# Transposing transfers by pairs and by whole weights in a kernel of a state-space branch and a linear-attention branch

## The chip, the cores and the metric

The kernel runs on one core of a Trainium2 chip. The metric is the device time of one execution in microseconds (us). The profile is that of one execution.

## The reference

The input `x` is 2048 rows (time) of 512 features. Two branches are computed from it and mixed by a gate per row. Cut to what matters:

```python
g = sigmoid((x * gate_w).sum(-1))
# A: a diagonal state-space model with 512 complex states
Bu = einsum("bld,pd->blp", x, B_bar)          # B_bar from B_re, B_im, Lambda, dt
h_t = Lam_bar * h_{t-1} + Bu_t                # over 2048 steps
y = 2 * einsum("blp,dp->bld", h, C).real + x * Dskip
# B: linear attention, 32 heads of 16
q, k, v = split(x @ wqkv)
phi(u) = concat(softmax(u @ w_phi), softmax(-u @ w_phi))      # 32 features per head
kv = phi(k)^T v;  z = sum(phi(k));  o = (phi(q) kv) / (phi(q) z + 1e-6)
out = g * y + (1 - g) * (o @ wo)
```

## The kernel before, in words

**Tiles and order.** The rows of `x` are cut into 16 tiles of 128 rows. A tile holds every eighth row, so that tile `ti` belongs to residue `r = ti // 2` of the time step modulo 8. `xT` holds `x` transposed, one transposing transfer per tile. Nothing is scheduled by the compiler: `ORDER` is a written list of tokens, and each token runs one generator up to its next `yield`. So the list fixes the order of instructions on TensorE (PE), VectorE (DVE), ScalarE (ACT) and the issuing order of SyncE (SP). `@n` gives the PSUM banks, `:D` sends an eviction to DVE instead of ACT. An engine runs its list strictly in order; semaphores make it wait for data.

**State-space branch.** `N` (`st_N`) loads B into `Bn`, real parts in partitions 0 to 63 and imaginary ones in 64 to 127, as eight blocks `t` of 64 states. `R{t}` (`st_BT`, L291) transposes one block into `BT`, four squares of 128x128, 128 KB of bf16. `g{r}{j}` (`st_g`, L614) multiplies `xT` by blocks `2j` and `2j+1` and evicts to `uv`. `z` scans along time, `h` (`st_h`, L685) adds the carried state and writes `HM`, `HE` and `H7`. C is read transposed by `C{0..7}` (`st_C`, L299), one quarter of C_re or C_im each, into `CA`, which lies in the space of `HM` before `h` writes it. `J` (`st_J`, L304) copies `CA` into `X1` and `X2`, in eight transfers, and `c{t}` (`st_c`, L603 and L607) scales and adds these into `C2r` and `C2i`. The two temporaries of a `c` sum, `mtmp[t % 4]`, lie in the space of `phT0[:, t % 4]`. `y` (`st_y`, L734) multiplies states by C.

**Attention branch.** `W` and `f` fold the key weight with `w_phi`; `Q{j}` (`st_Q`, L295) transposes a quarter of the query weight out of DRAM into `WTq`, `w` (L434) folds it. `k`, `v`, `q` are the projections. The features are made in groups of up to four tiles: `x`, `n` and `e` (maxima, minima, exponentials), then `s` (`feat_sum`: sums, logarithms, ratio). For queries, `feat_sum` also transposes the features into `phT`: per tile one transposing transfer of eight squares (256 KB, L579), or, for tiles 14 and 15 (`PH_PE`), PE transposes. The query groups are A (tiles 0 to 3, tokens `sA`, target `phT0`) and 1 to 3 (tokens `S1` to `S3`). `o{n}` (L753) multiplies the transposed features of tile n by the key-value sums in two halves, ACT takes logarithm and exponential of the denominators (`ld`, `rd`), DVE writes `on` (L761), and SP transposes `on` into `oT` (128 KB, L775; the last four on PE). `t{n}` (L782) adds `oT` times `wo` to the open sum of `y{n}` and sends the tile out (L790). The tokens run in the order o0, o2, o3, o1, then 4 to 9, 11, 10, 12, 14, 13, 15.

**SP's queue.** Nearly all transfers are issued by SP, in the order of the list. Each holds one of eight semaphores, handed round, so that a transfer waits for the one eight before it.

Of the kernel before, what the change touches and what calls it, by code (L numbers as in the profile page):

```python
# [31 lines left out]
g30 g50 n4 x4 e3 e3 g41@0 g50 n4 R7 s2 g21@4 s2 g70 s2 C7 e3 g31@3 e3 s3 g62@2 C4 g70 g70 z0 g11@7 a2 z0 s3 g41 z0 a2
a2 s3 C6 g21 g62 C2 C1 g11 g11 C0 J0 w0@6 w1@0 J2 J2 a2 g22@4 J0 w2@2 x4 s3 J1 g31 w1 w0 w3@7 g22 g31 z0 z0 z0 s3 w2
s3 n4 z0 z0 w3 g61@0 g51@6 g51 g61 g02@4 g51 e4 g02 g71@3 g71 g71 g71 q3@2 s3 g12@7 g12 e4 q2@0 z0 g12 z1 q3 q1@6 q1
q0@4 q2 z1 z0 h50@3 z1 z1 g42@7 q0 z1 z1 v10@26 h50 xA z1 h10@0 e4 e4 z1 g42 nA s4 g32@4 v10 g32 a3 g52@3 g32 h60@7 c2
xA s4 c4 O g52 xA c4 R6 z1 z1 v9@26 s4 h10 g52 nA g72@4 g72 c4 h60 v9 a3 J3 g03@3 v11@26 c2 c2 s4 g72 g72 c0 c0 nA
g63@0 z2 z2 v12@74 a3 nA v11 a3 xA g03 z2 z2 z2 z2 xA nA s4 J3 g63 g23@2 c5 s4 v12 g23 h51@6 g13@3 g13 g13 z2 z2 c0 z2
z2 eA g43@0 g43 eA v14@74 v14 J1 h51 s4 g33@2 g33 h52@3 g33 h12@0 g53@6 eA g53 g53 h12 h11@7 h11 h52 eA sA g73@4 g73
g73 g73 v13@26 v13 q10@0 z3 c6 z3 c5 sA z3 z3 v15@73 z3 a4 a4 a4 v15 z3 q10 q5@4 a4 Y z3 h31@0 q5 sA h30@4 z3 q9@2 h31
q13@6 h31 q9 h33@0 h61@7 Y q13 h30 sA sA c5 h62@3 z3 z3 h30 h61 sA Y Y h22@5 q4@2 h62 q4 h33 q15@6 q11@7 h22 h20@4 h20  # L40
h32@2 h32 sA sA c1 q11 h13@1 h13 h32 q14@3 h40@5 h33 c3 h53@7 h42@4 sA h42 h53 c1 c1 sA h21@2 c3 h21 q6@0 q6 q15 c6
q7@1 h63@4 h63 q8@7 h03@0 c3 q7 c6 h40 sA c7 h41@6 h41 y6@2 c7 h03 h03 h43@4 h43 y2@1 h02@5 c7 sA h23@6 h23 h01@0
h00@4 END q8 G X1 y6 y6 q14 y2 N1 X1 h00 h00 N1 y2 h02 h02 X1 N1 G h01 o0@6 y0@7 o0 o0@3 h01 o2@4 o2 X1 o2@5 o2 o2 N1
y5@6 o0 y3@0 X1 N1 y5 X2 o0 o1@4 E1 o2 y0 o2 o0 E1 E1 E1 X2 y1@5 y1 y3 y3 o1 G N2 X2 N2 X2 o0 N2 X2 o3@3 o3 o3@4 S1 o3
o3 G S1 N2 S1 t2 o3 S1 o3 t2 t2:A q12@3 q12 N2 S1 S1 o1@4 o1 o1 o1 o1 S1 S1 E2 S1 y0 y4@1 y9@3 y8@4 y8 y8 X3 E2 E2 S1
S1 S1 N3 X3 E2 t3 X3 X3 X3 S2 N3 t0 t0 t0:A S2 t3 S2 y1 t1 t1 y5 y9 y9 o4@7 o4 o4@0 o4 y4 o4 o4 o4 o5@5 o5 o5@7 o5 o5
y13@0 S2 S2 o6@5 o6 o6@7 o6 o6 y13 N3 y7@5 y7 N3 y7 y13 o5 S2 S2 N3 E3 o5 o6 o6 S2 S2 E3 E3 o7@7 o7:D y4 t4 t4:D t5
o7@7 S2 S2 E3 S3 t5 S2 S3 S3 o7 o7 o7 t6 y11@1 y11 o7 t6 o8@6 o8 o8@7 o8 o8 S3 S3 o8 y12@2 o9@6 o9 o9@7 o8 y11 y12 y12
y10@6 o9 o9 o9 o11@7 o11 o9 S3 S3 y10 y10 o11@7 t7 o11 o11 t7 t8 S3 S3 o11 o11 S3 t8 S3@7 S3:D S3@5 S3 t9 t9 t1:A
o10@4 y15@7 o10:D o10@5 o10:D t8 o10 o10 o10 y15 o12@4 o12:D o12@3 t4 o14@5 o12 o12 o12 t5 o14 t11 o14@4 o14:D o14 o14  # L50
t11 y14@3 t9:A o13@5 o13 o12@4 o12:D y14 o13@1 o13 o13 o15@4 o15:D o15@5 o15 o15 t12 t3:A t10 o13 o13@1 o15 t6:A t11
# [19 lines left out]
def kernel(  # L71
# [145 lines left out]
    WTq = HMf[:, 0:KT * D].rearrange("p (k d) -> p k d", k=KT)  # L217
    CA = HMf[:, KT * D:KT * D + 2 * PT * D].rearrange("p (a k d) -> p a k d", a=2, k=PT)
    BD = pAC.tile([P, HG, P], BF16, name="BD")
    BT = pAC.tile([P, KT, NT2, P], BF16, name="BT")  # L220
    T2c = pAC.tile([P, PT, NC], BF16, name="T2c")
    T2s = pAC.tile([P, PT, NC], BF16, name="T2s")
    uv = [pAC.tile([P, 7, 2, NC], BF16, name=f"uv{j}") for j in range(PT)]
# [63 lines left out]
        nc.sync.dma_start(out=Bn[ri * 64:(ri + 1) * 64, :, :], in_=(A_B_re, A_B_im)[ri].rearrange("(t p) d -> p t d", p=64))  # L287
        yield

    def st_BT(t):  # L290
        nc.sync.dma_start_transpose(out=BT[:, :, t, :], in_=Bn[:, t, :])  # L291
# [252 lines left out]
    def feat_sum(p, L, nm, small, ph=None, row0=0):  # L544
        EE = live["EE", p]
        E5 = EE.rearrange("p l hh s (f hl) -> p l (hh s) f hl", f=Dh)
        sm = small().tile([P, 4, 2 * NB, 1, 4], F32, name=f"sm{nm}1", bufs=2)[:, 0:L]
        yield from tree(small(), E5, L, ALU.add, f"sm{nm}", ("sm", p), last=sm, groups=2 * NB)
        lg = small().tile([P, 4, 2 * NB, 1, 4], F32, name=f"lg{nm}", bufs=1)[:, 0:L]
        aexp(out=lg, in_=sm, func=ACT.Ln)  # L550
        yield
        if ph is None:
            rc = small().tile([P, 4, 2 * NB, 1, 4], BF16, name=f"rc{nm}", bufs=2)[:, 0:L]
            aexp(out=rc, in_=lg, func=ACT.Exp, scale=-1.0)
            yield
# [12 lines left out]
        yield
        dst = ph()
        for u in range(L):  # L570
            if row0 + u in PH_PE:
# [7 lines left out]
            nc.sync.dma_start_transpose(out=dst(u), in_=EE[:, u].rearrange("p m s f -> p (m s f)"))  # L579
# [30 lines left out]
    def st_g(r, j):  # L610
        pg = bank([P, 2, NC], F32, "pgq")
        for h in range(2):
            for kt in range(KT):
                MM(out=pg[:, h, :], lhsT=BT[:, kt, 2 * j + h, :], rhs=xT[:, kt, r * NC:(r + 1) * NC], start=(h == 0 and kt == 0),  # L614
                   stop=(r % 2 == 0 and kt == KT - 1), skip_group_check=True)
# [249 lines left out]
```

## Time and profile before

| What | Value |
|---|---|
| time, median of 2 runs | 156.8 us (156.07 and 157.53) |
| span of the profiled execution, first to last instruction | 153.7 us |
| busy: PE, DVE, ACT, POOL | 145.5, 131.0, 136.7, 12.9 us |
| transposing transfers on SP: xT, BT, Q, C, phT, oT | 16, 8, 4, 8, 14, 12 |
| instructions | 3412 |

The profiled execution's own time is not listed apart from the two runs. The span lies 2.4 us below the faster and 3.8 us below the slower of them, and 3.1 us below their median. In the profile, PE is matmuls and PEld the loading of their weights, which overlaps with them; `L753` is a line of the kernel; `phT<-EEq` is an instruction that writes `phT` and reads `EEq`; SPq is an issue by SP.

### The profile page before, as it was taken

To read this page: it belongs to the slowest core of one execution; us is meant where nothing else is said; L and a number is where in the kernel's file an instruction comes from. 1 tells how busy PE (TensorE), PEld (TensorE's weight loads), DVE (VectorE), ACT (ScalarE), POOL (GpSimd) and SP (SyncE) were. 2 spreads that over 40 slices of the span, in tenths; PEclk is the share of its full clock that TensorE was granted. 3 is DMA by queue.
4 is the path that set the end of the run, shared out by engine and by line. 5 is a ranking of instruction groups with operands and counts; after the bars stand their busy time and mean duration, and the time that the engine had idled before them with its cause. 6 is when DMAs were issued, how large, how long until landed. Compare 5 with 4: busy or idle time off the path is not lost.

```text
span 153.7 us, 3412 instructions
## 1 busy us (share of the span) xinstructions
PE 145.5 (95%) x1238; PEld 99.7 (65%) x1254; DVE 131.0 (85%) x302; ACT 136.7 (89%) x322; POOL 12.9 (8%) x43
## 2 busy tenths in 40 slices
PE   7799999999999999999999999999999899999990
PEld 7656665886899858889876565554545455555550
DVE  3599999999999999999999999999999858445510
ACT  3599999999999999999999999999798897577672
POOL 8258800000000000000000000000000000000000
PEclk9999999999999999999999999999999999999998
DMA  4788995544474379960000006603139938667633
GB/s 117 162 220 121 213 171 102 102 86 92 101 102 100 80 146 205 237 133 0 2 4 2 0 0 134 125 18 68 33 82 118 215 80 194 141 118 172 211 123 102
DMA packets 48737, 17.03 MB, mean 111 GB/s; under 512 B 42064, under 2 KB 48720, under 8 KB 48720
## 3 DMA queue, kind: packets, MB, share of 16 engines
q1 hardware_dynamic: 47008, 15.36, 50.6%
q10 hardware_dynamic: 1552, 1.44, 2.9%
q8 instruction: 10, 0.16, 0.5%
q0 software_dynamic: 160, 0.01, 0.2%
q14 instruction: 7, 0.06, 0.1%
HBM read 2.64 MB, written 2.10 MB: 31 GB/s over the span
## 4 chain that ended last, share of the span: by engine, by line
ACT 48%; PE 31%; DMA 8%; DVE 6%; issue 3%; POOL 2%; ACTq 0%; POOLq 0%
PE py L734 12%; ACT EEk L140 12%; ACT uv L121 9%; PE py L782 6%; ACT vx L121 5%; PE pq L478 5%; ACT Xq L121 5%; ACT phT L603 4%; PE ph L685 3%; ACT va L121 3%; DMA phT<-EEq 3%; DMA oT<-on 3%; PE pn L753 2%; DMA vec_n<-in_A_log_dt_dram 2%; ACT EEq L140 2%
## 5 line engine op out<-in xcount | busy, mean ns | idle before, releaser
L614 PE MATMUL pgq<-xT,BT 128*128 128x256 bf16 x256 | 31.5, 272 | 0.0
L614 PEld LDWEIGHTS <-BT 128*128 128x128 bf16 x256 | 24.7, 98 | 3.5
L140 ACT ACTIVATE EEk<-EEk 128x1024 bf16<-128x1024 bf16 x20 | 21.3, 1099 | 0.0
L478 PEld LDWEIGHTS <-xT 128*128 128x128 bf16 x128 | 12.2, 97 | 11.0 <-issue 0.2
L121 ACT CAST uv<-pgq 128x512 bf16<-128x512 f32 x28 | 16.7, 638 | 0.0
L492 PE MATMUL pv<-Wv,xT 128*128 128x256 bf16 (+1 forms) x128 | 16.5, 273 | 0.1
L478 PE MATMUL pq<-Wq,xT 128*128 128x512 bf16 x60 | 15.2, 379 | 0.2
L782 PE MATMUL py<-Wo,oT 128*128 128x512 bf16 x59 | 14.7, 379 | 0.6 <-DMA oT<-on 0.3
L478 PE MATMUL pk<-Wk,xT 128*128 128x512 bf16 x60 | 14.9, 379 | 0.2
L492 PEld LDWEIGHTS <-xT 128*128 128x128 bf16 x128 | 12.5, 98 | 3.1 <-issue 0.2
L786 ACT ACTIVATE ot<-py,G 128x512 bf16<-128x512 f32 x15 | 9.8, 684 | 2.9 <-PE py L782 2.4
L140 ACT ACTIVATE EEq<-EEq 128x1024 bf16<-128x1024 bf16 x12 | 11.8, 1084 | 0.3 <-DVE EEq L535 0.3
L603 ACT ACTIVATE phT<-X,dgB 128x512 bf16<-128x512 bf16 x16 | 11.1, 751 | 0.0
L140 ACT ACTIVATE ld<-pn 128x16 f32<-128x16 f32 x32 | 6.4, 204 | 5.2 <-PE pn L753 5.0
L121 ACT CAST vx<-pv 128x256 bf16<-128x256 f32 x32 | 10.7, 435 | 0.0
L121 ACT CAST nu<-pn 128x256 bf16<-128x256 f32 x26 | 10.0, 400 | 0.0
L556 DVE TENSOR_TENSOR EEk<-EEk,rck 128x4096 bf16<-128x4096 bf16 (+1 forms) x5 | 9.3, 1860 | 0.1
L121 ACT CAST Xq<-pq 128x512 bf16<-128x512 f32 x16 | 9.0, 604 | 0.4 <-PE pn L753 0.4
L782 PEld LDWEIGHTS <-oT 128*128 128x128 bf16 x64 | 5.7, 98 | 5.7 <-DMA oT<-on 0.5
L753 PEld LDWEIGHTS <-phT 128*128 128x128 bf16 x128 | 6.4, 97 | 4.6 <-DMA phT<-EEq 1.3
L761 DVE TENSOR_TENSOR on<-nu,rd 128x512 bf16<-128x512 bf16 x16 | 6.6, 422 | 2.6 <-ACT rd L140 2.1
L519 DVE TENSOR_TENSOR smk<-smk 128x512 bf16<-128x512 bf16 (+4 forms) x18 | 8.1, 449 | 0.1
(179 smaller groups left out, 322.9 us busy)
## 6 DMA issues: line engine op xcount, KB each, us to landing
X<-HM SPq DMA_DIRECT2D x8, 256.0 KB, 4.7
out_dram<-ot SPq DMA_DIRECT2D x9, 128.0 KB, 2.2
out_dram<-ot ACTq DMA_DIRECT2D x7, 128.0 KB, 2.0
C2r<-in_B_wqkv_dram ACTq DMA_DIRECT2D x2, 256.0 KB, 3.5
Wv<-in_B_wqkv_dram SPq DMA_DIRECT2D x1, 512.0 KB, 4.0
Bn<-in_A_B_im_dram SPq DMA_DIRECT2D x1, 512.0 KB, 5.5
Bn<-in_A_B_re_dram SPq DMA_DIRECT2D x1, 512.0 KB, 5.9
Wo<-in_B_wo_dram SPq DMA_DIRECT2D x1, 512.0 KB, 5.9
```

Of the source, the lines that this page charges most:

```text
L121: nc.scalar.copy(out=out_ap, in_=in_ap)
L140: ins = nc.scalar.activation(**kw)
L478: MM(out=pt[:], lhsT=xT[:, kt, ti * P:(ti + 1) * P], rhs=W[:, kt, :], start=(kt == 0), stop=(kt == KT - 1))
L492: MM(out=pv[c][:], lhsT=xT[:, kt, ti * P:(ti + 1) * P], rhs=Wvg[:, kt, c * hd:(c + 1) * hd + c], start=(kt == 0), stop=(kt == KT - 1))
L519: VT(out=dst, in0=cur[:, :, :, 0:n, :], in1=cur[:, :, :, n:2 * n, :], op=op)
L556: VT(out=E5, in0=E5, in1=rc.to_broadcast([P, L, 2 * NB, Dh, 4]), op=ALU.mult)
L603: nc.scalar.mul(out=t_, in_=x_, mul=c_)
L614: MM(out=pg[:, h, :], lhsT=BT[:, kt, 2 * j + h, :], rhs=xT[:, kt, r * NC:(r + 1) * NC], start=(h == 0 and kt == 0), stop=(r % 2 == 0 and k ...
L734: MM(out=py[:], lhsT=hs(r, t, slice(a * P, (a + 1) * P)), rhs=C2B[t], start=(t == 0), stop=False)
L753: MM(out=pn[:, 4 * m:4 * m + 4, :].rearrange("p h e -> p (h e)"), lhsT=ph[:, 4 * hf + m, :], rhs=KVm[:, 4 * hf + m, :], start=(m == 0), st ...
L782: MM(out=py[:], lhsT=oT[:, g, :], rhs=Wo[:, g, :], start=False, stop=(g == HG - 1))
L786: nc.scalar.mul(out=ot[:], in_=py[:], mul=G[:, ti:ti + 1])
```

## The change

- BT is transposed by pairs of blocks: one transfer of eight squares for `2j` and `2j+1`. Its layout becomes `[P, NT2, KT, P]`; each square read by PE is as contiguous as before.
- C is transposed in two transfers (C_re, C_im), each of sixteen squares, 512 KB.
- The query weight is transposed in one transfer of sixteen squares.
- Query features are transposed by two tiles, sixteen squares, 512 KB: 0-1, 2-3, 4-5, 6-7, 8-9, 10-11 and 12-13.

That is 4 + 6 + 3 + 7 = 20 transposing transfers fewer, with the same bytes. In the list, tokens of transfers that no longer exist are left out, and everything else keeps its order. Q stands where the first quarter stood, the BT pairs where R0, R3, R5 and R7 stood, C_im where its first quarter stood and C_re where its first quarter stood. A feature pair stands where the transfer of its later tile or a place between stood: 0-1 in the place of tile 1, 2-3 in that of tile 3, 12-13 in that of tile 13. With that, SP issues `oT` of tile 11 ahead of the pair 12-13, where it stood between 12 and 13; the other pairs keep their neighbours on SP. The lists of PE, DVE and ACT keep their order.

```diff
-    BT = pAC.tile([P, KT, NT2, P], BF16, name="BT")
+    BT = pAC.tile([P, NT2, KT, P], BF16, name="BT")
...
-    def st_BT(t):
-        nc.sync.dma_start_transpose(out=BT[:, :, t, :], in_=Bn[:, t, :])
+    def st_BT(j):
+        nc.sync.dma_start_transpose(out=BT[:, 2 * j:2 * j + 2].rearrange("p t k c -> p (t k) c"), in_=Bn[:, 2 * j:2 * j + 2, :].rearrange("p t d -> p (t d)"))
         yield
-    def st_Q(j):
-        nc.sync.dma_start_transpose(out=WTq[:, j, :], in_=B_wqkv[:, j * P:(j + 1) * P])
+    def st_Q():
+        nc.sync.dma_start_transpose(out=WTq, in_=B_wqkv[:, 0:D])
         yield
-    def st_C(kt, ri):
-        nc.sync.dma_start_transpose(out=CA[:, ri, kt, :], in_=(A_C_re, A_C_im)[ri][:, kt * P:(kt + 1) * P])
+    def st_C(ri):
+        nc.sync.dma_start_transpose(out=CA[:, ri], in_=(A_C_re, A_C_im)[ri])
         yield
...
-            nc.sync.dma_start_transpose(out=dst(u), in_=EE[:, u].rearrange("p m s f -> p (m s f)"))
-            yield
+            if u % 2 == 0:
+                nc.sync.dma_start_transpose(out=dst(slice(u, u + 2)).rearrange("p u m c -> p (u m) c"), in_=EE[:, u:u + 2].rearrange("p u m s f -> p (u m s f)"))
+                yield
...
-                MM(out=pg[:, h, :], lhsT=BT[:, kt, 2 * j + h, :], rhs=xT[:, kt, r * NC:(r + 1) * NC], start=(h == 0 and kt == 0),
+                MM(out=pg[:, h, :], lhsT=BT[:, 2 * j + h, kt, :], rhs=xT[:, kt, r * NC:(r + 1) * NC], start=(h == 0 and kt == 0),
```

More of the change, by code (lines that the diff above doesn't have):

```diff
@@ L32 @@
[L32 to L51, printed above, removed]
@@ L52 @@
-o14@4 o13:D t7 t10 t10 y15 t12 t12 o15@5 o15 y14 o14:D t13 t14 t14 t14 t13 t13 t15 t15 t15:A
+k6@7 L e0 n1 n1 x1 n1 l13 k6:D v4@14 x1 l14 v1@03 v1 k10@6 n1 x2 v4 n2 n2 n2 x2 e0 s0 x2 v3 v7@70 v7 l15 k8@3 v2@14
+v6@25 s0 s0 k9@7 k12@0 x2 Q e1 s0 v2 v6 s0 k11@1 s0 e1 M k11 k8 D k10 k9 R1 k12 g40@4 g40 s0 s1 g00@2 g00 n2 a0@51 a0
+v5@36 v5 s1 R2 x2 v8@70 v8 C1 s1 s1 s1 s1 g60@4 n2 x3 s1 g60 g30@2 x3 n3 x3 n3 g10@3 g20@6 e2 e2 e2 e2 x3 a1 a1 n3
+k15@7 g10 g10 k15 x3 n3 g20 k14@0 k14 s2 n3 s2 k13@4 g01@3 k13 n4 s2 g30 g01 x4 s2 x4 n4 x4 g50@7 g70@6 g30 g50 n4 x4
@@ new lines @@
+e3 e3 g41@0 g50 n4 R3 s2 g21@4 s2 g70 s2 e3 g31@3 e3 s3 g62@2 C0 g70 g70 z0 g11@7 a2 z0 s3 g41 z0 a2 a2 s3 g21 g62 g11
+g11 J0 w0@6 w1@0 J2 J2 a2 g22@4 J0 w2@2 x4 s3 J1 g31 w1 w0 w3@7 g22 g31 z0 z0 z0 s3 w2 s3 n4 z0 z0 w3 g61@0 g51@6 g51
+g61 g02@4 g51 e4 g02 g71@3 g71 g71 g71 q3@2 s3 g12@7 g12 e4 q2@0 z0 g12 z1 q3 q1@6 q1 q0@4 q2 z1 z0 h50@3 z1 z1 g42@7
+q0 z1 z1 v10@26 h50 xA z1 h10@0 e4 e4 z1 g42 nA s4 g32@4 v10 g32 a3 g52@3 g32 h60@7 c2 xA s4 c4 O g52 xA c4 z1 z1
+v9@26 s4 h10 g52 nA g72@4 g72 c4 h60 v9 a3 J3 g03@3 v11@26 c2 c2 s4 g72 g72 c0 c0 nA g63@0 z2 z2 v12@74 a3 nA v11 a3
@@ new lines @@
+xA g03 z2 z2 z2 z2 xA nA s4 J3 g63 g23@2 c5 s4 v12 g23 h51@6 g13@3 g13 g13 z2 z2 c0 z2 z2 eA g43@0 g43 eA v14@74 v14
+J1 h51 s4 g33@2 g33 h52@3 g33 h12@0 g53@6 eA g53 g53 h12 h11@7 h11 h52 eA sA g73@4 g73 g73 g73 v13@26 v13 q10@0 z3 c6
+z3 c5 sA z3 z3 v15@73 z3 a4 a4 a4 v15 z3 q10 q5@4 a4 Y z3 h31@0 q5 sA h30@4 z3 q9@2 h31 q13@6 h31 q9 h33@0 h61@7 Y q13
+h30 sA sA c5 h62@3 z3 z3 h30 h61 sA Y Y h22@5 q4@2 h62 q4 h33 q15@6 q11@7 h22 h20@4 h20 h32@2 h32 sA sA c1 q11 h13@1
+h13 h32 q14@3 h40@5 h33 c3 h53@7 h42@4 h42 h53 c1 c1 sA h21@2 c3 h21 q6@0 q6 q15 c6 q7@1 h63@4 h63 q8@7 h03@0 c3 q7 c6
@@ new lines @@
+h40 c7 h41@6 h41 y6@2 c7 h03 h03 h43@4 h43 y2@1 h02@5 c7 sA h23@6 h23 h01@0 h00@4 END q8 G X1 y6 y6 q14 y2 N1 X1 h00
+h00 N1 y2 h02 h02 X1 N1 G h01 o0@6 y0@7 o0 o0@3 h01 o2@4 o2 X1 o2@5 o2 o2 N1 y5@6 o0 y3@0 X1 N1 y5 X2 o0 o1@4 E1 o2 y0
+o2 o0 E1 E1 E1 X2 y1@5 y1 y3 y3 o1 G N2 X2 N2 X2 o0 N2 X2 o3@3 o3 o3@4 S1 o3 o3 G S1 N2 S1 t2 o3 S1 o3 t2 t2:A q12@3
+q12 N2 S1 S1 o1@4 o1 o1 o1 o1 S1 S1 E2 y0 y4@1 y9@3 y8@4 y8 y8 X3 E2 E2 S1 S1 N3 X3 E2 t3 X3 X3 X3 S2 N3 t0 t0 t0:A S2
+t3 S2 y1 t1 t1 y5 y9 y9 o4@7 o4 o4@0 o4 y4 o4 o4 o4 o5@5 o5 o5@7 o5 o5 y13@0 S2 S2 o6@5 o6 o6@7 o6 o6 y13 N3 y7@5 y7
@@ new lines @@
+N3 y7 y13 o5 S2 S2 N3 E3 o5 o6 o6 S2 E3 E3 o7@7 o7:D y4 t4 t4:D t5 o7@7 S2 E3 S3 t5 S2 S3 S3 o7 o7 o7 t6 y11@1 y11 o7
+t6 o8@6 o8 o8@7 o8 o8 S3 S3 o8 y12@2 o9@6 o9 o9@7 o8 y11 y12 y12 y10@6 o9 o9 o9 o11@7 o11 o9 S3 S3 y10 y10 o11@7 t7
+o11 o11 t7 t8 S3 o11 o11 S3 t8 S3@7 S3:D S3@5 S3 t9 t9 t1:A o10@4 y15@7 o10:D o10@5 o10:D t8 o10 o10 o10 y15 o12@4
+o12:D o12@3 t4 o14@5 o12 o12 o12 t5 o14 t11 o14@4 o14:D o14 o14 t11 y14@3 t9:A o13@5 o13 o12@4 o12:D y14 o13@1 o13 o13
+o15@4 o15:D o15@5 o15 o15 t12 t3:A t10 o13 o13@1 o15 t6:A t11 o14@4 o13:D t7 t10 t10 y15 t12 t12 o15@5 o15 y14 o14:D
@@ L53 @@
+t13 t14 t14 t14 t13 t13 t15 t15 t15:A
 """
@@ L795 @@
     st = {"V": st_V(), "V2": st_V2(), "U": st_U(), "P": st_P(), "P2": st_P2(), "P3": st_P3(), "P4": st_P4(), "B": st_B(), "gw": st_gw(),
-          "M": st_M(), "D": st_D(), "L": st_L(), "G": st_G(), "Y": st_Y(), "END": st_END(), "NR": st_N(0), "NI": st_N(1), "O": st_O()}
+          "M": st_M(), "D": st_D(), "L": st_L(), "G": st_G(), "Y": st_Y(), "END": st_END(), "NR": st_N(0), "NI": st_N(1), "O": st_O(), "Q": st_Q(), "C0": st_C(0), "C1": st_C(1)}
     for n in range(8, NTI):
@@ L799 @@
     for j in range(4):
-        st.update({f"W{j}": st_W(j), f"Q{j}": st_Q(j), f"C{2 * j}": st_C(j, 0), f"C{2 * j + 1}": st_C(j, 1), f"f{j}": st_f(j), f"w{j}": st_w(j), f"i{j}": st_i(j), f"z{j}": st_z(j),})
+        st.update({f"W{j}": st_W(j), f"f{j}": st_f(j), f"w{j}": st_w(j), f"i{j}": st_i(j), f"z{j}": st_z(j),})
+        st[f"R{j}"] = st_BT(j)
         for r in range(8):
@@ L805 @@
     for t in range(NT2):
-        st.update({f"R{t}": st_BT(t), f"c{t}": st_c(t)})
+        st[f"c{t}"] = st_c(t)
     for k in range(4):
```

4 lines of the change are left out of this document (removed).

## The prediction, made before the changed kernel was run

> **What bounds the kernel now.** I read the page first (busy shares, GB/s in 40 slices, the chain that ended last), then the waits, then stretches of 4 us, then single transfers.
>
> ```profile
> span 153.7 us, 3412 instructions
> PE 145.5 (95%) x1238; PEld 99.7 (65%) x1254; DVE 131.0 (85%) x302; ACT 136.7 (89%) x322; POOL 12.9 (8%) x43
> GB/s 117 162 220 121 213 171 102 102 86 92 101 102 100 80 146 205 237 133 0 2 4 2 0 0 134 125 18 68 33 82 118 215 80 194 141 118 172 211 123 102
> ACT 48%; PE 31%; DMA 8%; DVE 6%; issue 3%; POOL 2%; ACTq 0%; POOLq 0%
> ```
>
> Next, of the waits (us in total, times, longest), the only one over 1 us on a transposed tile; then three stretches with the busy time of PE, PEld, DVE, ACT and POOL, the clock, DMA share and GB/s.
>
> ```profile
> PEld L753 <- DMA phT<-EEq: 1.3, 2, 0.9
> 100.00:104.00 4.00, 3.94 (x33) 2.13 (x33) 4.00 (x9) 4.00 (x16) 0.00 (x0) 1.00 0.05 12
> 116.00:120.00 4.00, 3.59 (x37) 1.97 (x35) 3.87 (x7) 3.03 (x9) 0.00 (x0) 1.00 1.18 135
> 140.00:144.00 4.00, 3.95 (x49) 2.46 (x49) 2.72 (x7) 2.88 (x13) 0.00 (x0) 1.00 0.80 223
> ```
>
> From 100 us on PE is nearly always busy, at the full clock, so a stall of PE goes to the end unless a later stall swallows it. The one wait of size for a transposed tile is that of the phT weight loads, 1.3 us in two; on PE itself it is 0.36 (the row stands below) and nearly all that the stretch at 116 lacks (3.59 of 4). A wait of 0.34 for oT follows at 134.7 (below). No engine waits for BT, Q's weight, C or X: they do not occur among the waits. So 0.7 us is what lighter queueing can give directly. The question is what twice as large transfers cost where tiles arrive just in time.
>
> **Price of one transfer.** The next rows are, by tile, SP's issues (shortest/median/longest ns) and, from the DMA view, the medians from issue to landing.
>
> ```profile
> L579 SPq DMA_TRANSPOSE phT<-EEq x10: 1242/1260/2604, 113.8 to 138.1; - x10
> L775 SPq DMA_TRANSPOSE oT<-on x12: 1190/1208/1951, 104.2 to 140.7; - x12
> oT<-on SPq DMA_TRANSPOSE x12, 2.4
> phT<-EEq SPq DMA_TRANSPOSE x10, 2.8
> phT<-EEk SPq DMA_TRANSPOSE x4, 3.1
> BT<-Bn SPq DMA_TRANSPOSE x8, 2.5
> ```
>
> oT is 128 KB (4 blocks of 128x128, bf16), phT 256 KB. The issue hardly grows (1208 to 1260 ns), so I take 1.3 us for 512 KB; its upper bound is an issue that goes by bytes, 2.5 us. Twenty issues fewer free 20 x 1.26 = 25 us of SP, which is not on the chain. Landing grows by 0.4 us for 128 KB more. No transfer of 512 KB is transposed here. By that step, 256 KB more take +0.8; if the page's best slice (237 GB/s, above) were the limit, 262 KB take 1.1. I take +1.0: phT pairs land after 3.8 us from EEq and 4.1 from EEk. The lower bound is +0.4 (one more such step).
>
> **What stays covered: BT, Q, C, X.** Timeline rows (start and length in us), and groups by tile with first and last start.
>
> ```profile
> 21.98 1.19 SPq L291 DMA_TRANSPOSE BT<-Bn  x1
> 26.06 0.53 PEld L614 LDWEIGHTS <-BT 128*128 128x128 bf16 x4
> 37.22 1.04 PE L614 MATMUL pgq<-xT,BT 128*128 128x256 bf16 x8
> L434 PE MATMUL pf<-BD,HM x16: 216/219/219, 46.5 to 49.1; 128*128 128x128 bf16 x16
> L603 ACT ACTIVATE phT<-X,dgB x16: 705/743/837, 62.5 to 96.4; 128x512 bf16<-128x512 bf16 x16
> ```
>
> The first pair of BT, 256 KB, issued at 21.98, lands 2.5 + 0.4 later, at 24.9, against the first use at 26.06: 1.2 us of cover, hidden by matmuls on xT. If a delay took it, PE would wait for the excess. The next pair leaves SP behind three loads of x and Q (about 28.5) and has until 37.2. Q has until 46.5. C and its copies X are done some 15 us earlier than needed, since ten issues before them are gone; ACT takes X at 62.5 without waiting now. So: 0, gain included. A loss needs a delay above 1.2 us at the first pair.
>
> **First term: pair 2-3 of the query features, group A.** Both tiles' space holds temporaries of the C sums (`mtmp`), so the pair waits for the last one, as tile 3 alone does now. Timeline rows, then rows of the DMA view.
>
> ```profile
> 93.60 1.23 SPq L579 DMA_TRANSPOSE phT<-EEk  x1
> 97.22 0.43 DVE L607 TENSOR_TENSOR C2i<-phT 128x512 bf16<-128x512 bf16 x1
> 97.67 1.23 SPq L579 DMA_TRANSPOSE phT<-EEk  x1
> 100.02 0.27 PEld L753 LDWEIGHTS <-phT 128*128 128x128 bf16 x4
> 100.90 0.63 PEld L753 LDWEIGHTS <-phT 128*128 128x128 bf16 x12
> q8 instruction: 1, 0.02, 28.7%
> q8 instruction: 1, 0.02, 3.2%
> BT<-Bn SPq DMA_TRANSPOSE x1, 4.0
> phT<-EEq SPq DMA_TRANSPOSE x1, 4.6
> ```
>
> Pair 0-1 takes the place of tile 1, issued at 93.60 (first row): it lands at 97.7, 2.3 us before tile 0 is wanted at 100.02, and costs nothing. Tile 2 now leaves ahead of the last C sum; as half of pair 2-3 it leaves at 97.67 and lands 4.1 later, at 101.8. The twelve weight loads from 100.90 on are four of tile 0 and then eight of tile 2, first wanted at about 101.2. PE stalls 0.6. Behind the waiting load stands all of PE's list, and ACT's logarithms and DVE's products wait for its results.
>
> The sixth row, from the DMA view of 100.2 to 100.4, is a load of 16 KB of instructions. The transpose issued at 97.67 lands at about 100.8 now, so that its data are nearly through by then; those of the pair, from the end of the issue at 98.9 to about 101.5, are hit in the middle. The last three rows price a hit: in the DMA view of 43.2 to 45.4, with one such load, a BT transpose took 4.0 instead of 2.5; the phT transpose issued at 115.15 took 4.6 instead of 2.8. That is 1.5 to 1.8; 0 if the load comes a little later. As the pair is half through, I take 1.2. First term: 0.6 + 1.2 = +1.8, bounds 0 (landing after 3.5, unhit) and 2.4 (0.6 + 1.8).
>
> [...]
>
> **Second term: the first pair of group 1.**
>
> ```profile
> 113.80 1.26 SPq L579 DMA_TRANSPOSE phT<-EEq  x1
> 118.13 0.34 PEld L753 LDWEIGHTS <-phT 128*128 128x128 bf16 x8
> q8 instruction: 1, 0.02, 3.8%
> 119.83 0.43 PE L753 MATMUL pn<-KVm,phT 128*128 128x68 bf16 x8 [0.36 <-DMA phT<-EEq]
> 121.09 0.31 PEld L753 LDWEIGHTS <-phT 128*128 128x128 bf16 x8 [0.47 <-DMA phT<-EEq]
> ```
>
> Tile 4 is wanted at 118.13, tile 5 at 119.8 (0.36 us late on PE), tile 6 at 121.1. The pair, issued at 113.80 like tile 4 today, lands at 117.6 unhit: no stall, and tile 5's 0.36 us is gained. But an instruction load falls between 116 and 119 (third row, DMA view of that stretch). Hit, the pair lands at 118.8 to 119.4: 0.7 to 1.3 of stall, less 0.36. If the first term moves PE but not the issue, the stall is covered. I take +0.3, bounds -0.4 and +0.9. The second pair then lands before 122, when PE, later by 2 us, asks for it.
>
> **Third term: group 3 and the end.**
>
> ```profile
> 134.72 1.69 PE L782 MATMUL py<-Wo,oT 128*128 128x512 bf16 x7 [0.34 <-DMA oT<-on]
> 135.19 0.42 DVE L761 TENSOR_TENSOR on<-nu,rd 128x512 bf16<-128x512 bf16 x1
> 135.47 1.25 SPq L579 DMA_TRANSPOSE phT<-EEq  x1
> 136.81 1.22 SPq L775 DMA_TRANSPOSE oT<-on  x1
> 138.12 1.27 SPq L579 DMA_TRANSPOSE phT<-EEq  x1
> 139.98 0.63 PEld L753 LDWEIGHTS <-phT 128*128 128x128 bf16 x12
> q14 instruction: 2, 0.02, 1.7%
> ```
>
> SP issues tile 12 now at 135.47, then oT of tile 11, then tile 13. In the changed program the pair takes the later place: behind oT, whose `on` ends at 135.61. That issue takes 1.2, so the pair leaves at 136.9 and lands 3.8 later, at 140.7, or 0.3 later still for the two small instruction loads between 136 and 139.2 (last row). Tile 12 is wanted at 139.98. Ahead of the oT that makes PE wait 0.34 at 134.72, SP has two issues of group 2 fewer, so it leaves up to 2.5 earlier; that wait goes, and tile 12 is wanted at 139.6. Stall 1.1 to 1.4, less 0.34: +0.8, bounds 0.2 and 1.3. Group 2 has no wait in the list now (the 1.3 in two are those of the second term), its first pair lands at most 1.0 later, and PE asks some 2 us later: 0.
>
> **Sum.** 1.8 + 0.3 + 0.8 = +2.9 us, span 153.7 to 156.6; bounds -0.2 and +4.6. The median of the two runs, 156.8, lies 3.1 above the span; I keep that: 159.7, that is 1.8% slower. From here on, 2% (3.1 us) is what a measurement can tell.
>
> **Rivals.**
> - *A larger transfer costs little more.* Each doubling adds 0.4, no load hits: tile 2 lands at 97.67 + 3.5 = 101.2, no stall; group 1 gains 0.36; group 3 lands at 140.1, stall 0.5 less 0.34. Sum -0.2: 156.6. For it: the step from oT to phT. Against it: the two hit transfers above.
>
>   [...]
> - *SP's queue is the limit.* Late issues, 1.26 each, are what PE waits for at 119.8 and 134.7. Place: SP between 113 and 137; price -0.36 - 0.34 = -0.7: 156.1, faster than before. It decides if pairs land within 3.5 us at 97.67 and 2.7 us at 136.9. Against it: phT of 256 KB already needs 2.8.
> - *The pair is not one cheap issue.* If SP's issue goes by bytes (2.5 us instead of 1.3), every pair lands 1.2 later: +3.6 at three places: 163.3. Then the change doesn't do what it says. Against it: 1208 against 1260 ns.
>
> **How the numbers follow.** Forecast 0.62 (its own range 157.2 to 161.4: the bounds, but the lower end moved up, as all three low together are the first rival), first rival 0.18, second 0.11, third 0.09. The range 156.9 to 161.9 leaves out nearly all of the second and third rivals (156.1 and 163.3) and a few hundredths of the first and the forecast, 0.2 in all, once half of the first is taken in by its uncertainty of half a us. Slower by over 2% (above 159.9): nearly half of the forecast and the third rival, 0.40. Faster by over 2% (below 153.7) needs 3.1 us where the rows show 0.7: 0.05, kept for what they do not show. Within: 0.55.
>
> **What would show it.** Right: phT comes in 7 transposes instead of 14, landing after 3.6 to 5.5 us, each issue near 1.3; PE's waits name phT<-EEk with about 1.8 us near 101, and phT<-EEq with about 1 near 120 and 142; no wait on BT or X. Wrong: pairs landing within 3.3 us, no wait at 101, or a wait for BT at 26.

## The result, and the profile after

The changed kernel took 162.59 us (161.45 and 163.73) against 156.8: a ratio of 1.0365 [1.0256, 1.0474]. Four further executions took 159.32 to 162.17, median 160.94, a ratio of 1.0248 [1.0201, 1.0295]; the middle of all six is 161.3. Slower, as forecast, but by 4 to 6 us instead of 2.9. The ratios leave out executions over 1.5% above the fastest of their kernel; some kernels below bring such executions themselves, so medians and ranges stand beside the ratios.

The page of the profiled execution (161.45 us), and its waits:

```profile
span 159.5 us, 3387 instructions
PE 146.0 (92%) x1254; PEld 99.2 (62%) x1254; DVE 131.2 (82%) x302; ACT 137.2 (86%) x322; POOL 12.8 (8%) x43
ACT 43%; PE 18%; DMA 16%; SPq 9%; DVE 9%; issue 3%; ACTq 0%
```

```profile
PEld L754 <- DMA phT<-EEq: 2.9, 3, 1.4
PEld L754 <- DMA phT<-EEk: 2.5, 1, 2.5
PE pn L754 <- DMA phT<-EEk: 2.3, 1, 2.3
PE pn L754 <- DMA phT<-EEq: 1.9, 2, 1.0
PEld L478 <- DMA xT<-in_A_x_dram: 1.7, 1, 1.7
PEld L783 <- DMA oT<-on: 1.1, 1, 1.1
```

The busy times are as before; the span is 5.8 us longer, and the chain's share of DMA is 16% instead of 8. PE waits for phT in four places and nowhere for BT or X. The transfers, from the views of tile phT on SP, of tile BT (each with its shortest, median and longest landing), and of the DMA queues from 98 to 104, 128 to 134 and 140.5 to 146 us:

```profile
L580 SPq DMA_TRANSPOSE phT<-EEq x5: 1593/1664/3368, 117.2 to 141.1; - x5
L580 SPq DMA_TRANSPOSE phT<-EEk x2: 1793/1880/1968, 94.7 to 98.8; - x2
DMA to landing us min/median/max: 3.9/4.6/6.1
L291 SPq DMA_TRANSPOSE BT<-Bn x4: 1232/1308/2222, 23.5 to 37.2; - x4
DMA to landing us min/median/max: 3.1/4.4/4.9
phT<-EEk SPq DMA_TRANSPOSE x1, 6.0
q8 instruction: 1, 0.02, 1.0%
phT<-EEq SPq DMA_TRANSPOSE x2, 3.9
out_dram<-ot SPq DMA_DIRECT2D x1, 128.0 KB, 3.9
out_dram<-ot ACTq DMA_DIRECT2D x1, 128.0 KB, 3.5
phT<-EEq SPq DMA_TRANSPOSE x1, 4.6
```

Seven phT transposes, as announced, but an issue takes 1.6 to 2.1 us instead of 1.3 (one took 3.4; before, the longest took 2.6). Left alone (group 2, 128 to 134), a pair lands after 3.9; with a load of 16 KB of instructions on the way (q8) the pair 2-3 takes 6.0; beside two writes of output tiles, which themselves take 3.5 and 3.9 where they take 2.1 elsewhere, the pair 12-13 takes 4.6. The BT pairs land after 3.1 to 4.9 us, and nobody waits for them.

**Where the time went.** All traces have the same 302 DVE instructions in the same order, so each can be set against the same one of before's profile. How much later it starts gives, step by step (us; "tile 12" holds the wait for the oT ahead of it too, which before's profile has with 0.34):

| profiled execution | at 100 us | group A | group 1 | tile 12 | after | at the end |
|---|---|---|---|---|---|---|
| changed | +1.15 | +2.34 | +0.64 | +1.42 | 0 | +5.55 |
| changed, again (e7) | +0.84 | +1.00 | +0.68 | +2.10 | +1.66 | +6.28 |

The first column is not made by the change: it comes with the wait of 1.44 us for xT that ends at 20.73, and the first merged transfer, BT, is issued only at 23.46. The executions of before beside the experiments had spans from 153.6 up, most 154.1 to 154.8, so its profiled one, with 153.7, was among the quickest. The wait stands in nine of the experiments' profiles too, all of kernels with the weights merged; why it came in them and not in before's is open, but e1, with the same weights, is level with before. The "after" column is new: behind the stall at tile 12 the granted clock falls. Stretches of e7 (busy time of PE, PEld, DVE, ACT, POOL, then the clock):

```profile
142.00:144.00 2.00, 0.41 (x2) 0.00 (x0) 0.65 (x2) 0.20 (x1) 0.00 (x0) 1.00 1.06 287
144.00:146.00 2.00, 0.98 (x14) 0.76 (x16) 0.42 (x1) 0.86 (x6) 0.00 (x0) 0.86 0.75 195
146.00:148.00 2.00, 2.00 (x9) 0.83 (x8) 1.00 (x3) 1.19 (x6) 0.00 (x0) 0.50 0.01 2
148.00:150.00 2.00, 2.00 (x17) 1.09 (x16) 0.70 (x2) 0.76 (x3) 0.00 (x0) 0.79 0.55 185
```

PE is idle for 2.4 us up to 144.80. Then the clock is 0.50 for 3.4 us: if it is either 1.00 or 0.50, the 0.86 means 0.56 us at half clock up to 146, and the 0.79 means 0.84 us from 148 on. Half of 3.4 us is 1.7, and the table has 1.66.

### The profile page after: what moved, and what is told of

It is laid out like the page before. It is cut to its first block, busy times and chain, and to the rows that moved or that the text cites. A ratio compares the mean times of both kernels' runs of the same rounds, so it can differ in the third digit from the quotient of the medians.

```text
span 159.5 us, 3387 instructions
## 1 busy us (share of the span) xinstructions
PE 146.0 (92%) x1254; PEld 99.2 (62%) x1254; DVE 131.2 (82%) x302; ACT 137.2 (86%) x322; POOL 12.8 (8%) x43
## 3 DMA queue, kind: packets, MB, share of 16 engines
q10 hardware_dynamic: 1552, 1.44, 2.8%
## 4 chain that ended last, share of the span: by engine, by line
ACT 43%; PE 18%; DMA 16%; SPq 9%; DVE 9%; issue 3%; ACTq 0%
ACT EEk L140 10%; ACT uv L121 8%; SPq L232 7%; PE py L735 6%; DMA phT<-EEq 6%; ACT Xq L121 5%; PE py L783 4%; DMA phT<-EEk 4%; ACT phT L604 3%; DMA xT<-in_A_x_dram 3%; ACT va L121 3%; ACT vx L121 3%; DMA oT<-on 3%; PE pk L478 3%; DVE Bn L690 2%
## 5 line engine op out<-in xcount | busy, mean ns | idle before, releaser
L783 PE MATMUL py<-Wo,oT 128*128 128x512 bf16 x64 | 15.6, 379 | 0.6 <-DMA oT<-on 0.6
L478 PE MATMUL pq<-Wq,xT 128*128 128x512 bf16 x64 | 15.8, 378 | 0.0
L754 PE MATMUL pn<-KVm,phT 128*128 128x68 bf16 x128 | 7.5, 194 | 4.4 <-DMA phT<-EEk 2.3
```

The lines of the kernel that those rows point to most:

```text
L478: MM(out=pt[:], lhsT=xT[:, kt, ti * P:(ti + 1) * P], rhs=W[:, kt, :], start=(kt == 0), stop=(kt == KT - 1))
L754: MM(out=pn[:, 4 * m:4 * m + 4, :].rearrange("p h e -> p (h e)"), lhsT=ph[:, 4 * hf + m, :], rhs=KVm[:, 4 * hf + m, :], start=(m == 0), st ...
L783: MM(out=py[:], lhsT=oT[:, g, :], rhs=Wo[:, g, :], start=False, stop=(g == HG - 1))
```

## The experiments

In kernels where the pairs are chosen by group, line 754 is 758 and 580 is 584 (single transposes 581). "Steps" are those of the table above.

**Which part of the change.** Four kernels: the weights alone, the pairs alone, all but group A's pairs, and all with the instruction loads moved.

```diff
 e1:  BT, C and Q as in the change, phT single
 e2:  phT by pairs; BT, C and Q as before
+e3:  PAIRED = ('G1', 'G2', 'G3')      # group A single
-e4:  F:28        # early filler matmuls
+e4:  F:12
```

> Only BT by pairs, C in two transfers and Q in one (13 transposes fewer); the query features are transposed tile by tile as before. Theory (the loss is the feature pairs; the 1.2 us that the changed kernel's profiled execution lost before 25 us is chance, since SP's list is the same up to there): ratio to before 0.99 to 1.01, no wait at 101 us, PE waits for oT or phT as before (about 0.7 us). Rival (the merged weight transfers delay the loads of x or slow the first half): 1.2 us slower or more, ratio 1.008 or above, with a wait for xT or BT near 20 to 30 us in its profile that before does not have.

Measured: 156.25 us, 0.9991 [0.9962, 1.002]. Thirteen of the twenty transfers fewer bring nothing and cost nothing.

> Only the query features by pairs (7 transposes fewer); BT, C and Q as before. Theory: all of the loss, some 4.5 us: ratio 1.025 to 1.037, with the wait for the pair 2-3 of group A at 2 us or more. Rival (merged weights carry part): ratio at most 1.02.

Measured: 160.19 (159.14 to 160.86), 1.024 [1.0189, 1.0291]; steps A +0.90, group 1 +0.64, tile 12 +1.67. A hair below the theory, and the loss is in the pairs. PE's wait for pair 2-3 was 0.9 us, where 2 or more was expected. The profiled execution (160.41) also has a half clock from 8.2 to 11.6 us, where the kernel is as before, and is 1.56 late at 100 us.

> The changed kernel, with group A's features tile by tile as before; groups 1 to 3 by pairs. Theory: the 2.3 us that PE waits for pair 2-3 go, and they stay gone, since PE has no idle time after it that could have covered them: some 2.4 us faster than the changed kernel, ratio to before 1.012 to 1.022. Rival (the later stalls grow by what the first no longer covers): less than 1 us of it comes back, ratio 1.028 or above.

Measured: 161.21 (159.34 to 163.03), 1.0251 [1.0171, 1.0331]: missed. A's step is gone (0), group 1 is +0.63, but tile 12 costs +2.41, and +1.66 behind it. Waits and stretches of e3:

```profile
PE pn L758 <- DMA phT<-EEq: 3.7, 2, 2.7
142.00:144.00 2.00, 0.15 (x5) 0.15 (x6) 0.00 (x0) 0.00 (x0) 0.00 (x0) 1.00 1.05 205
144.00:146.00 2.00, 2.00 (x21) 1.08 (x19) 0.85 (x2) 1.25 (x7) 0.00 (x0) 0.68 0.35 112
146.00:148.00 2.00, 2.00 (x12) 1.04 (x11) 0.85 (x2) 1.23 (x5) 0.00 (x0) 0.50 0.20 66
148.00:150.00 2.00, 2.00 (x23) 1.17 (x22) 0.42 (x1) 1.04 (x7) 0.00 (x0) 0.97 0.39 131
```

The half clock lasts 3.4 us again (0.68 is 1.28 us, 0.97 is 0.12). PE, not held up in A, stands 2.7 us at tile 12.

> The changed kernel with 12 instead of 28 filler products at its start, which are there to keep PE running while the first loads arrive and whose sums nobody reads: 32 PE instructions fewer, so each load of 16 KB of PE's instructions comes some 2 us later in PE's list. Theory (an instruction load in the middle of a transpose costs it 1.5 us or more): pair 2-3 of group A lands 4.1 to 4.5 us after its issue instead of 6.0, PE waits 0.5 to 0.9 for it instead of 2.3, and the whole is 1 to 2 us faster than the changed kernel unless the load then hits another transpose that PE waits for. Rival (the pair takes 6.0 us by its size or by what else SP sends): landing and wait stay as they are, within 0.3 us.

Measured: 161.17 (all within 0.6), 1.0306 [1.0274, 1.0337]. The mechanism holds, the gain does not come: pair 2-3 lands 4.27 after its issue, A's step is +0.59, group 1 becomes a gain of 0.52, but tile 12 then costs +2.77 and +1.31 behind it, at half clock again. What is saved early is lost at tile 12.

**Tile 12, and the groups one by one.**

```diff
 e5:  order of S3, o11
-... t7 t8 S3 o11 o11 S3 t8 S3@7 ...
+... t7 t8 S3 S3 o11 o11 t8 S3@7 ...
+e6:  PAIRED = ('G1', 'G2')     # weights as in the change
+e9:  PAIRED = ('A',)           # the same
+e10: PAIRED = ('G3',)          # the same
+e11: PAIRED = ('G1', 'G2', 'G3'), order as e5
```

> The changed kernel with one token moved: the transfer for tiles 12 and 13 stands ahead of the transpose oT of tile 11 on SP's queue (where the token of tile 12 alone stood before), instead of behind it. Theory (the stall at group 3 is the late issue plus the larger transfer, and its cost is the wait of 2.5 to 3.5 us that also makes the clock fall): the wait at tile 12 shrinks by about 1.3 us, to 0 to 1.5 us, the granted clock stays at 1.00 between 140 and 150 us, and the ratio to the kernel before falls from 1.036 to 1.012 to 1.025. Rival (the size of the transfer alone sets the stall): the wait stays near 2.5 us or more and the ratio at 1.03 to 1.04.

Measured: 160.4 (158.14 to 161.85), 1.0248 [1.019, 1.0307]. In the profiled execution (158.14) the stall is gone. Timeline rows of e5:

```profile
137.57 1.62 SPq L584 DMA_TRANSPOSE phT<-EEq  x1
139.32 1.22 SPq L780 DMA_TRANSPOSE oT<-on  x1
142.14 0.63 PEld L758 LDWEIGHTS <-phT 128*128 128x128 bf16 x12
```

The pair leaves at 137.57, lands 4.5 later at 142.10, and the weight loads at 142.14 wait for nothing: tile 12 costs -0.24. But other executions of e5 stay at 159.4 to 161.9 with mean clocks of 0.987 to 0.993, so something loses 1.3 to 3.7 us in them that this profile does not show (e14 and e15, below, show what group A can lose).

> B, C and Q's weight in merged transfers as in the change; pairs of phi-token transposes in groups 1 and 2 only, single ones in groups A and 3. Theory (the loss is of the stalls in groups A and 3, group 1 costs 0.64 us, group 2 nothing): ratio 0.998 to 1.008. Rival (every pair costs through its issue on SP's queue, 1.6 to 2.0 us against 1.2, whichever group it is in): ratio 1.012 to 1.020, half of the change's loss.

Measured: 157.35, 1.006 [1.0035, 1.0084]; group 1 +0.63, group 2 and the rest -0.25. As the theory has it.

> The changed kernel again, word for word, for its spread and its clock. Theory (three stalls, and a clock that falls to half after the last one where that is long): ratio 1.028 to 1.040; the wait at tile 12 is 1.0 to 3.0 us, and where it is over 2.5 us the granted clock is near 0.5 for some 3 us behind it and the run is at the upper end, 162.5 us or more; where it is below 2 us the clock stays at 1.00 and the run is near 161. Rival (the clock has nothing to do with the stall): the clock falls also where the stall is short, or stays where it is long.

Measured: 160.94 (159.32 to 162.17), 1.0248 [1.0201, 1.0295]. The profiled execution, 162.17, has PE's idle time of 2.4 us and the half clock; the other three, at mean clocks of 0.996 to 0.999, took 159.3 to 161.2. The first profile (PE's longest wait for EEq 1.0) has no fall at tile 12.

> B, C and Q's weight in merged transfers, the phi-token transposes single in all groups as before, and 12 instead of 28 filler matmuls at one early place (nobody reads what they write), which moves the loads of PE's instructions about 2 us against the transposes. Theory (in the kernel with the merged weights alone, the waits that are left, 0.76 and 0.46 us on phi-token transposes of group 1 and 1.33 us on an oT, are transfers hit by an instruction load): the waits shrink by 0.5 to 1.5 us together and the ratio is 0.990 to 0.998. Rival (the hits are only moved to other transfers): ratio 0.998 to 1.004.

Measured: 157.24, 1.003 [1.0002, 1.0058]: missed. With all tiles single, other transfers are waited for (one phT wait of 1.85 us, one oT of 0.91); that the moved loads hit these was not shown.

> B, C and Q's weight in merged transfers, pairs of phi-token transposes in group A alone (tiles 2 and 3), single ones elsewhere. Theory (group A's stall costs 0.1 us where no instruction load meets the transfer or all of its hiding is used, and up to 2.3 us where one does): ratio 1.001 to 1.015, runs spread by up to 2 us, no stretch at half clock. Rival (the excess of the changed kernel sits in group A): ratio 1.02 or more.

Measured: 160.28 (158.46 to 161.19), 1.0132 [1.0079, 1.0184]. A alone costs 2 to 4 us; the two slowest executions have a mean clock of 0.989. Median against median (156.84) it is a ratio of 1.022.

> B, C and Q's weight in merged transfers, the pair of phi-token transposes in group 3 alone (tiles 12 and 13, behind the oT of tile 11), single ones elsewhere. Theory (a stall of 1.4 to 2.8 us at tile 12, and 1.3 to 1.7 us more in the runs whose clock falls behind it): ratio 1.009 to 1.027; runs with a mean clock of 0.99 or less lie 1 us or more above those at 0.995 or more. Rival (the three groups' stalls share one cause, and one pair alone costs at most its own price of the prediction, 0.8 us): ratio 1.000 to 1.006.

Measured: 157.31 (156.76 to 160.29), 1.0033 [1.0, 1.0065]. Nearer to the rival: tile 12 costs +1.20, but group 1, without pairs, gains 0.34, for a reason that stays open, and only two of ten executions (159.57 and 160.29, clocks 0.988 and 0.984) are high. With single transposes in groups 1 and 2, the pair's issue stands better against the demand. Rows of e10 and, in the next fence, of e7:

```profile
137.00 1.65 SPq L584 DMA_TRANSPOSE phT<-EEq  x1
141.42 0.56 PE L758 MATMUL pn<-KVm,phT 128*128 128x68 bf16 x12 [0.95 <-DMA phT<-EEq]
```

```profile
139.53 1.72 SPq L580 DMA_TRANSPOSE phT<-EEq  x1
144.80 0.56 PE L754 MATMUL pn<-KVm,phT 128*128 128x68 bf16 x12 [2.39 <-DMA phT<-EEq]
```

From the issue to the moment when PE stands are 3.5 us in e10 (137.00 to 140.47) and 2.9 in e7 (139.53 to 142.41); the landing takes 4.4 and 5.2. So the prices of groups don't simply add.

> The changed kernel with group A's transposes single and the pair of tiles 12 and 13 ahead of the oT of tile 11. Theory (what is left is group 1's 0.6 us): ratio 1.002 to 1.010 and a mean clock of 0.993 or more in every run. Rival (with group A in pairs, the kernel with the early pair had runs of 159.4 to 161.9 us beside its profiled 158.1; if that excess comes of group 3 and not of group A, it is still there): ratio 1.015 to 1.03, some runs below 0.99 in clock.

Measured: 157.62 (157.0 to 159.79), 1.0048 [1.0014, 1.0082]. Against e3 (1.0251) one token's move is worth 3.2 us by the ratios, and without A's pairs all but one execution (159.79) stay below e5's slower three. The time is as the theory has it, the clock is not: two of ten have 0.985 and 0.986. The profiled one of these (159.01) has its half clock in the start, where the kernel is as before; a low mean clock alone does not tell where it fell:

```profile
5.00:10.00 5.00, 3.24 (x34) 2.46 (x33) 3.17 (x19) 3.64 (x9) 0.12 (x1) 0.90 0.70 169
10.00:12.00 2.00, 2.00 (x6) 0.76 (x5) 2.00 (x7) 1.49 (x3) 1.92 (x6) 0.50 0.89 188
```

**The clock.** Fillers in the stall at tile 12, and two more executions of the kernel with pairs in A alone (e14, e15: e9 word for word).

```diff
+e12: F@4:24      # 24 filler matmuls into a free bank
 e12: o12@4
```

> The changed kernel with 24 filler matmuls on TensorE (nobody reads what they write) right ahead of the matmuls of tile 12 that wait for the pair, some 1.6 us of work in the stall. Theory (the clock falls because TensorE stands idle for some 2.4 us or more): the stall itself stays (work behind it starts at the same time or up to 0.6 us later), the granted clock stays at 1.00 between 140 and 152 us and the mean clock is 0.993 or more in every run; the ratio is 1.016 to 1.028, below that of the changed kernel in the same state of the wait, and no run lies above 162 us. Rival (the clock falls for another reason, such as the burst of work behind the stall): runs with a mean clock below 0.99 as before, ratio 1.027 to 1.04.

Measured: 162.11 (160.4 to 163.51), 1.0296 [1.0243, 1.0349]. Local yes, whole no. In the profiled execution (160.4) tile 12 costs +2.12, as much as in e7, and nothing follows. Stretches of e12:

```profile
142.00:144.00 2.00, 1.51 (x25) 1.33 (x23) 0.43 (x1) 0.00 (x0) 0.00 (x0) 1.00 1.05 285
144.00:146.00 2.00, 1.41 (x21) 0.93 (x22) 0.58 (x2) 1.07 (x6) 0.00 (x0) 1.00 0.64 167
146.00:148.00 2.00, 2.00 (x21) 1.11 (x18) 1.54 (x4) 1.64 (x6) 0.00 (x0) 1.00 0.19 66
```

That alone does not show that the fillers kept the clock up, since the changed kernel's first profile has no fall there either. And the time is no better: two of six executions are still at 0.986 and 0.989, so the clock fell somewhere in them, and two at 1.000 took 161.97 and 162.25, which no fall explains. What loses the time in them is open.

> The kernel with the pair in group A alone, word for word, for another look at its clock. Theory (the executions 2 us above the profiled one, at a mean clock of 0.989, lose it in a stretch at half clock behind a stall, at tile 2 near 105 us or in the start near 10 us): if the time is over 160 us, the granted clock shows such a stretch; if it is near 158.5 us, none. Rival: a slow execution without any stretch at half clock.

> The same kernel once more, and the same theories: over 160 us with a stretch at half clock behind a stall, or near 158.5 us with none; rival: slow without such a stretch.

Measured: 160.62 and 160.64, both at a mean clock of 0.989. PE waited 2.3 us at tile 2 in e14, as in e9's profile, and here the clock fell behind it. Stretches of e14, and then of e9:

```profile
102.00:104.00 2.00, 0.00 (x0) 0.00 (x0) 2.00 (x3) 0.67 (x2) 0.00 (x0) 1.00 0.04 9
104.00:106.00 2.00, 1.71 (x13) 0.82 (x14) 0.61 (x2) 1.37 (x8) 0.00 (x0) 0.81 0.00 0
106.00:108.00 2.00, 2.00 (x6) 0.73 (x5) 1.79 (x7) 2.00 (x4) 0.00 (x0) 0.50 0.28 66
108.00:110.00 2.00, 2.00 (x12) 0.90 (x11) 1.83 (x5) 2.00 (x4) 0.00 (x0) 0.84 0.30 66
```

```profile
104.00:106.00 2.00, 1.64 (x15) 0.94 (x16) 0.61 (x2) 1.30 (x8) 0.00 (x0) 1.00 0.00 0
106.00:108.00 2.00, 2.00 (x15) 0.94 (x14) 1.79 (x6) 2.00 (x4) 0.00 (x0) 1.00 0.28 65
```

Group A's step is +4.02 in e14 and +3.93 in e15, against +2.34 in e9. That is the second place of the fall, and e9's high executions have the mean clock of e14.

Why the same stall of 2.3 us brings the fall once and not the other time can be read from the traces. Within each of the eighteen profiles, all changes of the granted clock lie whole steps of 3.413 us apart. The next rows cut e14 and e9 at these steps (e9's last change is at 154.60 us, 15 steps after 103.40):

```profile
101.83:105.24 3.41, 1.10 (x17) 0.62 (x14) 2.53 (x3) 1.45 (x8) 0.00 (x0) 1.00 0.05 10
105.24:108.65 3.41, 3.41 (x10) 1.18 (x9) 2.69 (x10) 3.41 (x8) 0.00 (x0) 0.50 0.17 38
```

```profile
99.98:103.40 3.42, 2.05 (x22) 1.38 (x20) 3.42 (x9) 2.75 (x8) 0.00 (x0) 1.00 0.68 129
103.40:106.81 3.41, 2.45 (x19) 1.28 (x20) 1.81 (x5) 2.12 (x9) 0.00 (x0) 1.00 0.00 0
```

In e14 the whole stall lies in one step: PE stands 2.31 of 3.41 us, and the next step is at half clock. In e9 the stall is cut in two, 1.37 and 0.96, and nothing falls; in the first profile of the changed kernel it is cut into 1.20 and 1.16. Up to 150 us the eighteen profiles have some 750 such steps and seven falls: five behind the five steps with the most idle time of PE (2.25 to 2.59: e15, e14, e7, e3, e4) and two in the start (1.56 in e2, 1.76 in e11); one step with 1.63 (e2, tile 12) and all with 1.48 or less brought none. So where a stall meets these steps is luck, and it decides over some 1.7 us.

**Group A: size or load.** And the whole change with both stalls moved.

```diff
+e13: PAIRED = ('A',), F:12
+e16: the whole change, order as e5, F:12
```

> As the kernel with the pair in group A alone, and 12 instead of 28 early filler matmuls (nobody reads what they write), so that the load of PE's instructions near 102.5 us comes some 2 us later. Theory (group A's cost is the meeting of the larger transfer with that load): the pair of tiles 2 and 3 lands 4.1 to 4.6 us after its issue instead of 6.0, PE waits 0 to 1 us instead of 2.3, ratio 1.000 to 1.007, against 1.013 with the pair in group A unshifted. Rival (the pair in A costs by its own size): ratio 1.010 to 1.018 again.

Measured: 157.79 (156.6 to 158.61), 1.007 [1.0039, 1.0101], no mean clock below 0.994. The wait is now

```profile
103.71 0.30 PEld L758 LDWEIGHTS <-phT 128*128 128x128 bf16 x8 [0.69 <-DMA phT<-EEk]
```

with the pair landing 4.26 after its issue and a step of +0.59. The load, not the size, makes the larger part of A's loss; the profiled execution also lost 0.8 in group 1, whose transposes are single; that the moved load now hits one of them was not shown.

> The whole change, all 20 transfers fewer, with the pair of tiles 12 and 13 ahead of the oT of tile 11 and 12 instead of 28 early filler matmuls (nobody reads what they write). Theory (the loss is where the pairs meet instruction loads and a late place on the queue, not the size or the count of the transfers): no wait of PE on phT over 1 us, ratio 1.000 to 1.008. Rival (the larger transfers cost their price wherever they stand): ratio 1.015 to 1.03.

Measured: 158.44 (157.38 to 159.33), 1.0132 [1.0096, 1.0168]: between the two forecasts; half of the loss is gone, not all. No wait on phT is over 1 us (A +0.59, group 1 -0.45, tile 12 0), no mean clock is below 0.995, but the wait has moved to the oT of tile 11, now behind the pair:

```profile
PEld L758 <- DMA phT<-EEq: 1.5, 2, 0.8
PEld L787 <- DMA oT<-on: 1.2, 1, 1.2
PEld L758 <- DMA phT<-EEk: 0.7, 1, 0.7
```

It costs +1.24 in the profiled execution (157.75); its other executions take up to 1.6 us more. Part of that lies ahead of the first instruction or behind the last: 159.33 belongs to a span of 156.5, where most executions have 2.0 between time and span. The cause of that part is open. Among the merged kernels e1 and, at the edge of its interval, e10 are level with the kernel before; none beats it.

## Why the prediction was right and where it was wrong

**Right.** The direction, the three places, and the covered part: BT, Q, C and X at 0 (e1), though the first BT pair landed after 3.1 us instead of 2.9 and others after up to 4.9. The unhit landing: 3.8 and 4.1 said, 3.9 and 4.3 measured. The unhit stall of A: 0.6 said, +0.59 in e4, e13 and e16. Group 1's sign: the hit pair, landing 5.5 us after its issue, costs (+0.64, said +0.3, bounds kept), the unhit one gains (-0.52 and -0.45, said -0.36). Group 2 at 0.

**First term: +1.8, measured +0.9 to +1.0, +2.3 or +4.0.** Its 0.6 supposes that tile 2 is usable only with its whole pair; no run shows that, as none tried a half. In the changed kernel the weight loads of tile 2 start at 104.88, 0.04 us after the whole pair has landed (98.82 + 6.02). The step that failed is "hit in the middle" and "as the pair is half through, I take 1.2". In before's profile the load starts 2.6 us after the issue at 97.67. In the changed kernel it starts 3.99 after the issue of the pair (102.81 against 98.82), just after PE has stopped, and 0.3 before an unhit pair would have landed. Even so late it costs 6.02 - 4.28 = 1.74, the upper end of the two rows used, so the price does not go by what is left of the transfer. The same offset, 3.96 to 4.01 us, cost 1.7 in e9, e14 and e15 too, but 0.3 to 0.4 in e2, e5, e7 (4.67, step +1.00) and e12; what decides between the two is open. With 12 fillers it is 4.17 to 4.24, 0.2 us later and not the 2 us expected, and costs nothing. So 1.8 lies between two outcomes, and its nearness to either is luck. The +4.0 contains the clock.

**Third term: +0.8, bounds 0.2 and 1.3, measured +1.4 to +2.8 (+1.2 in e10).** The step that failed is the landing, 3.8 plus 0.3 for small instruction loads (the 0.3 was the author's estimate, no run prices such a load): the pair takes 4.4 to 5.4, where the pairs of group 2 take 3.9. The sum left out the two output tiles that ACT and SP write at the same time. That these make the difference is argued from the times alone; no run moved them, and an oT is in flight ahead of the pair too. The gain of 0.34 at oT came in e7, but in the profiled execution PE waited 0.64 there. The place behind oT was the right reason: e5 and e11 undo it and the stall goes, though the pair still takes 4.5 and 4.9.

**Not forecast: the clock.** "At the full clock" was read from before, where PE waits at most 0.36 us for a transfer from 100 us on, and kept for a kernel in which it stands 2 to 3 us. A fall costs 1.3 to 1.7 us, at tile 12 (e3, e4, e7) or behind A (e14, e15: 4.0 less 2.34). In these five profiles the clock is 0.50 for 3.4 us behind a step of 3.41 us in which PE stood 2.25 to 2.59 us. Such a fall would have been a rival: 2.9 + 1.5 gives 161.2. It also marks what lies beyond the stated range: of the six executions of the changed kernel, the two beyond 161.9 (162.17 and 163.73) have a mean clock of 0.986, and the four at 0.996 to 0.999 took 159.32 to 161.45. For 163.73, which has no profile, where the clock fell is not known.

**The issue** of 512 KB takes 1.6 to 2.1 us instead of 1.3, which goes a quarter to two thirds of the way to the third rival's 2.5; but its price, pairs landing 1.2 later, did not come, since an unhit landing is as forecast. The first two rivals fall: the quickest pairs landed after 3.9 us, where they needed 3.5 or less (2.7 at tile 12).

Added up, the profiled execution has 2.34 + 0.64 + 1.42 = 4.4 where the sum had 2.9; e7 has 1.00 + 0.68 + 2.10 + 1.66 = 5.4. The 3.1 us that the forecast adds to the span takes in the table's first column: in all listed executions of before and of the changed kernel, time and span lie 1.9 to 2.2 apart (161.45 and 159.5), so some 1.1 of it is that before's profiled execution was quick. What stays open is the spread among executions without a profile, for which only times and mean clocks are known.

## What to carry to other kernels

Merge transfers that are waited for late (13 fewer here: 0.9991 of the time, e1); where PE asks for the first part of a transfer as soon as it is there, the merge delays that part by the whole (the weight loads of tile 2 did not wait before; with the pair they waited 0.69 us in e13 and, with a load on the way, 2.45 in the changed kernel), and the just-in-time rows of the profile tell which is which. Price a larger transfer with everything else under way in its window (instruction loads, output writes of other queues), as it is exposed for longer: a phT pair took 3.9 us left alone, 6.0 with a load of 16 KB, 4.6 beside two output writes. And price a stall of over 2 us on PE with the half clock that may follow (here 0.50 for 3.4 us, worth 1.3 to 1.7 us, behind stalls of 2.3 to 3.0 us in e3, e4, e7, e14 and e15).

## What the runs showed of the hardware

- A granted clock of 0.50 for 3.4 us followed PE idle times of 2.4, 2.7 and 3.0 us (e7, e3, e4); after 2.3 us it came in e14 and e15 and not in e9 or the first profile; after 1.8 (e2) it did not.
- In each of the eighteen profiles the granted clock changed only at steps of 3.413 us (before: its changes at 5.50 and 152.27 us lie 43 of them apart); up to 150 us the half clock followed every step in which PE stood 2.25 us or more, none with 1.48 or less, and two of three with 1.56 to 1.76.
- One 16 KB load of instructions that started 4.0 us after the issue lengthened a transpose of 512 KB by 1.74 us (4.28 to 6.02) in four profiles (changed, e9, e14, e15) and by 0.3 to 0.4 in four others (e2, e5, e7, e12).
- The issue of a transposing transfer: 1.2 us for 128 KB and 1.26 for 256 KB (before, medians of oT and phT), 1.6 to 2.1 for 512 KB of phT (changed; one took 3.4).
